# A fused attention, Fourier-mixing and feed-forward kernel: its planner gets a fitted transfer model, port rules and new durations

## Chip, core and metric

The kernel runs on 1 core of one Trainium2 chip. The metric is the device time of one execution in microseconds; the time of the kernel before is the median of three runs.

## What is computed

The reference, cut to what matters (batch 8, 8 heads, sequence 576, head size 64; x is [8, 576, 512]):

```python
rel = pos[:, None] - pos[None, :]
mask_plain = (rel >= 0) & (rel < 32)                       # heads 0 to 3
mask_dil = (rel >= 0) & (rel < 128) & (rel % 4 == 0)       # heads 4 to 7
scores = where(mask, q @ k.T / 8, -1e9)
x = softmax(scores) @ v                                    # heads side by side: [8, 576, 512]
u = x + real(fft(fft(x, axis=1), axis=2))
un = (u - mean(u)) / sqrt(var(u) + 1e-6)                   # over the last axis
out = u + maximum(un @ w_ch1, 0) @ w_ch2                   # 512 -> 2048 -> 512
```

## The kernel before

**Stages.** For each of 8 batches, attention runs in 12 small steps of two 96-row blocks for a pair of heads (`attend`, L513): TensorE multiplies queries and keys (L522), VectorE adds the mask and takes the row maximum in one operation (L530), ScalarE takes the exponential (L536), TensorE transposes it (L549) and multiplies it with the values (L556), VectorE divides by the sums (L564 to L568). `store` sends the result to folded scratch tensors in DRAM, `xsp` and `xsm` (L603). `mix` (L657) loads those folded tiles back (L675, L684, tiles `x0` to `x3`, `xt0`, `xt1`) and does the two Fourier transforms as products with constant cosine and sine tables `seq`, `chn`, `tail` and `alt`; float32 numbers are split into a high and a low part, and three products of parts make one. `normalise` (L614) makes the layer norm and stores u with its mean and scale.

The feed-forward layer has two parts. During attention, `fill` works through the first 5 of 16 slices of the hidden layer, two token tiles at a time, with `up` (L935) and `down` (L951), and `keep_part` stores the sums in `parts`. After that, 9 blocks of 512 tokens do the other 11 slices: `load_blocks` (L1065) turns the tokens (L1033, a VectorE transpose), makes four combinations (L1077) and splits seven operands into high and low parts in `xb` (L1087 on ScalarE, L1090 on VectorE or GpSimd); `two_tiles` (L1237) makes products by a seven-product scheme (L1209); `down` adds them up; `finish` (L972) adds the stored part, scales, adds u and writes the output rows. Weights come as 64-bit words that VectorE converts in five operations each (L866, L869, L872, L875, then L882 for the low part); those of the first slices are converted during attention, those of pair 3 and later during block 0.

**What sets the order.** Nothing in the code above runs in the order in which it is written. `Plan.add` records each step with an engine, a cost in us, a priority and its tiles; `Plan.run` (L235) then simulates the engines and the DMA queues with these costs and takes, whenever an engine is free, the ready step of the lowest priority. The instructions are emitted in that order, so each engine's queue is fixed by it, and at run time an engine goes through its queue in order and waits at each step. The priorities are the constants `P_...` and the step of the batch: 12 units for each batch. SyncE issues nearly all loads and stores, GpSimd those of the tables and the indirect ones. Before, a transfer is modelled like this:

```python
dma = max(dma, end + 0.65) + got.nbytes / 3.0e5
done = dma + 2.8
```

and GpSimd's table loads have no dependence but a time, `at=T_SEQ` or `T_CHN`, that exists in the plan alone; `start` (L450) writes them behind nothing on GpSimd's queue (L481, L483, L485, L486).

Of the kernel before, what the change touches and what calls it, by code (L numbers as in the profile page):

```python
# [173 lines left out]
class Op:  # L174
    __slots__ = ("eng", "cost", "fn", "prio", "bufs", "after", "waits", "ready", "start", "num", "nbytes")


class Plan:
# [1146 lines left out]
```

## Time and profile before

| | before |
|---|---|
| median of three runs (lowest, highest) | 1114.68 us (1114.53, 1117.69) |
| the profiled execution | 1114.71 us |
| its span | 1112.9 us |
| TensorE (PE) busy | 1064.3 us, 7066 matmuls |
| VectorE (DVE) busy | 726.0 us, 2318 instructions |
| ScalarE (ACT) busy | 522.2 us, 1331 instructions |
| GpSimd (POOL) busy | 288.7 us, 341 instructions |

The span is the time from the first to the last thing that the profiler saw; the execution's own time is 1.8 us longer. Busy times of the engines overlap. The granted clock (PEclk) is the share of full speed that TensorE was allowed: at 1.00 it runs at 2.4 GHz, and a mean between 0.5 and 1.00 says that it spent a part of the stretch at 1.2 GHz. DMA share is the mean busy share of the core's 16 DMA engines; overlapping transfers can bring it above 1.

### The profile page before, as it was taken

Reading aid. Unit: us, or ns where it says so; the run is one execution under the profiler, and the core shown is the slowest. Engines: PE = TensorE matmul, PEld = TensorE weight load, DVE = VectorE, ACT = ScalarE, POOL = GpSimd, SP = SyncE. Lnnn points to the kernel's source line nnn. Section 1 sums busy time; section 2 is a strip of 40 time slices with the busy share of each in tenths; the row PEclk is TensorE's granted clock in tenths of the full one; section 3 lists DMA queues with packets and bytes.
Section 4 is the critical chain, followed back from the end, with each engine's and each line's share of the span. In section 5 each row is a group of like instructions: output and inputs, shape, how many; then the busy total and the mean of one; then the engine's idle time right before and its main releaser. Section 6 shows DMA issues by size and latency. Waiting matters only on the chain.

```text
span 1112.9 us, 20217 instructions
## 1 busy us (share of the span) xinstructions
PE 1064.3 (96%) x7066; PEld 944.7 (85%) x7066; DVE 726.0 (65%) x2318; ACT 522.2 (47%) x1331; POOL 288.7 (26%) x341
## 2 busy tenths in 40 slices
PE   5799999999999999899989899999999999999997
PEld 3667888889898988899978798999998989899986
DVE  4789988777867878867769853536363545454523
ACT  3587756646554735334435443333333333333431
POOL 2015465443434344400040321121202120212200
PEclk9699999999999999999989999999999999999999
DMA  9667567756565344345523360505050504041211
GB/s 310 175 205 223 160 192 194 210 144 183 162 171 152 115 129 131 104 133 153 133 95 102 79 162 1 152 1 152 1 152 1 138 15 124 30 103 50 92 61 39
DMA packets 104310, 137.05 MB, mean 123 GB/s; under 512 B 9656, under 2 KB 62328, under 8 KB 104208
## 3 DMA queue, kind: packets, MB, share of 16 engines
q1 hardware_dynamic: 100624, 126.85, 40.6%
q0 software_dynamic: 3040, 8.09, 2.4%
q8 instruction: 56, 0.92, 0.4%
q10 hardware_dynamic: 544, 0.82, 0.2%
q14 instruction: 46, 0.38, 0.1%
HBM read 97.92 MB, written 37.80 MB: 122 GB/s over the span
## 4 chain that ended last, share of the span: by engine, by line
PE 80%; DVE 12%; DMA 3%; issue 2%; POOL 1%; ACT 1%; SPq 0%; DVEq 0%; ACTq 0%; POOLq 0%
PE sc L951 14%; PE ff L1209 13%; PE mix L1209 8%; PE ff L951 6%; PE ff L935 6%; PE pt L951 6%; PE av L951 6%; PE sc L522 6%; PE av L556 4%; PE mix L784 2%; PE mix L738 2%; PE pt L549 2%; PE pt L935 2%; DVE pm L530 1%; DMA ut<-in_w_dram 1%
## 5 line engine op out<-in xcount | busy, mean ns | idle before, releaser
L536 ACT ACTIVATE pm<-pm,mx 96x128 f32<-96x128 f32 x384 | 130.3, 394 | 54.2 <-DVE mx L530 50.6
L522 PE MATMUL sc<-kb,tq 128*96 128x256 f32 x384 | 110.1, 407 | 16.7 <-DMA kb<-in_k_dram 7.7
L1225 ACT COPY s<-ff 128x256 f32<-128x256 f32 x135 | 50.3, 374 | 159.2 <-PE ff L1209 158.9
L935 PE MATMUL ff<-ut,wa 128*128 128x256 f32 x780 | 109.0, 289 | 3.7 <-DVE h L943 3.6
L530 DVE CUSTOM_DVE_ANT_0 pm<-sc,mask_sb 96x128 f32<-96x128 f32 x384 | 92.8, 278 | 24.5 <-PE sc L522 23.9
L951 PE MATMUL sc<-wa,h 128*128 128x512 f32 x420 | 104.4, 391 | 0.0
L935 PEld LDWEIGHTS ff<-ut,wa 128*128 128x128 f32 x780 | 98.7, 192 | 5.7 <-DVE h L943 4.3
L951 PE MATMUL ff<-wa,h 128*128 128x512 f32 x390 | 93.8, 392 | 0.0
L556 PEld LDWEIGHTS av<-vt,ptsb 128*96 128x96 f32 x768 | 79.5, 170 | 16.2 <-issue 4.6
L1077 POOL TENSOR_TENSOR ut<-ut 128x512 f32<-128x512 f32 x36 | 50.6, 1426 | 160.3 <-DVE ut L1033 81.3
L556 PE MATMUL av<-vt,ptsb 128*96 128x65 f32 x768 | 84.4, 253 | 6.1 <-DVE xt L568 4.4
L951 PEld LDWEIGHTS sc<-wa,h 128*128 128x128 f32 x420 | 76.0, 188 | 13.8
L522 PEld LDWEIGHTS sc<-kb,tq 128*96 128x96 f32 x384 | 58.3, 174 | 30.6 <-DVE kb L465 7.7
L951 PE MATMUL sc<-wd,h 128*128 128x512 f32 x324 | 83.7, 393 | 0.0
L951 PEld LDWEIGHTS ff<-wa,h 128*128 128x128 f32 x390 | 71.6, 188 | 13.8
L1033 DVE STREAM_TRANSPOSE ut<-ut 128x512 f32<-128x512 f32 (+1 forms) x76 | 71.4, 980 | 13.6 <-DMA ut<-us 13.6
L1256 DVE TENSOR_TENSOR c<-s,s 128x256 f32<-128x256 f32 x45 | 22.2, 494 | 88.1 <-ACT s L1225 88.0
L1209 PEld LDWEIGHTS ff<-xb,pair 128*128 128x128 f32 x540 | 73.8, 188 | 6.4 <-ACT s L1225 0.7
L1209 PE MATMUL ff<-xb,pair 128*128 128x256 f32 x540 | 76.4, 280 | 0.5 <-ACT s L1225 0.5
L1090 POOL TENSOR_TENSOR xb<-ut,xb 128x512 fp32r<-128x512 f32 x27 | 36.9, 1367 | 132.1 <-ACT xb L1087 132.1
L1230 ACT ACTIVATE h<-row 128x256 fp32r<-128x256 f32 x90 | 37.5, 417 | 64.2 <-DVE row L1246 37.3
L989 POOL DMA_INDIRECT ut<-us,flip_sb x20 | 19.9, 996 | 183.8 <-DMA ut<-us 107.5
(158 smaller groups left out, 2312.2 us busy)
## 6 DMA issues: line engine op xcount, KB each, us to landing
vt<-in_v_dram SPq DMA_DIRECT2D x32, 390.0 KB
ut<-in_w_dram SPq DMA_DIRECT2D x20, 512.0 KB
us<-uc SPq DMA_DIRECT2D x36, 257.0 KB
tq<-in_q_dram SPq DMA_DIRECT2D x32, 288.0 KB
part<-row SPq DMA_DIRECT2D x36, 256.0 KB
ut<-us SPq DMA_DIRECT2D x36, 256.0 KB
ut<-part SPq DMA_DIRECT2D x36, 256.0 KB
kb<-in_k_dram SPq DMA_DIRECT2D x62, 144.0 KB
```

Of the source, the lines that this page charges most:

```text
L522: nc.tensor.matmul(sc()[:QB, 256 * n:256 * n + 256], lhsT=tq()[:, cols], rhs=kb()[:, :, keys], start=True, stop=True,)
L530: nc.vector.tensor_tensor_reduce(pm()[:, i], sc()[:QB, KB * i:KB * i + KB], mask_sb()[:, masks[blocks[i // 2]]], -0.125, 3.0e38, ALU.add, ...
L536: add("ACT", 0.295, lambda i=i: nc.scalar.activation(out=pm()[:, i], in_=pm()[:, i], func=AF.Exp, bias=mx()[:, i:i + 1], scale=-1.0), ((mx ...
L556: add("PE", 0.16, lambda i=i: nc.tensor.matmul(av()[:QB, 65 * i:65 * i + 65], lhsT=pt()[:, i], rhs=vt()[:, i % 2, blocks[i // 2]], start=T ...
L935: nc.tensor.matmul(z()[:, :n_tok], lhsT=wf()[:, a, kk], rhs=ut()[:, p, kk], start=(kk == 0 and n == 0), stop=(kk == KT - 1 and n == 2),)
L951: nc.tensor.matmul(acc(), lhsT=h()[:, a, P * s:P * s + P], rhs=wf()[:, p], start=(first and n == 0), stop=(last and n == 2),)
L1033: nc.vector.transpose(out=o[back], in_=x[:, g])
L1077: add("POOL", pool(C), lambda: nc.gpsimd.tensor_tensor(out=made(i)(), in0=x(), in1=y(), op=ALU.subtract), (*done, *((raw, ("s", j)) for j ...
L1090: add(eng, (pool if eng == "POOL" else dve)(C), lambda j=j, get=get, lo=lo: lo.tensor_tensor(out=xb()[:, j, 1], in0=get(), in1=xb()[:, j, ...
L1209: nc.tensor.matmul(z()[:, lo:lo + TOK1], lhsT=ap()[:, a, kk], rhs=xb()[:, j, p, kk], start=(start and k == 0), stop=(stop and k == 6 * len ...
L1225: add("ACT", act(TOK1), lambda: nc.scalar.copy(out=s(), in_=src()[:, :TOK1]), (src,), (s,), SOON - 1)
L1230: add("ACT", act(TOK1), lambda: nc.scalar.activation(out=h()[:, 0], in_=z(), func=AF.Relu), need, ((h, 0),), SOON)
```

## The change

The planner gets other numbers. A transfer now starts 0.83 us (SyncE, ScalarE) or 3.6 us (GpSimd) after its issue, moves 260 GB/s in place of 300, and lands 1.02 + 1.5 us later; rows of 2 KB count 0.52 of their bytes. Steps marked `port` (VectorE operations with two inputs in SBUF, and everything that GpSimd computes) exclude each other in the plan. Durations are changed (a VectorE transpose 1.0 in place of 0.6, matmuls and others by some per cent), and all priorities get new values.

Four things are changed beyond the order. Each table load of GpSimd gets a VectorE memset of one element of its tile ahead of it, on which it then depends. In the first block (XB = 1) `load_blocks` puts all combinations and splits on VectorE. In `finish` VectorE first makes u + part x scale, which doesn't need the accumulator, and then one scale-and-add from the accumulator, in place of an add of accumulator and part and a scale-and-add. SyncE's issue cost in the plan goes from 0.5 to 0.46.

```diff
-P_QK0, P_V0 = -8.0, -7.0
-P_ST, P_FD, P_WD, P_ST0, P_FD0, P_SPAN0, P_SPAN1 = -4.0, -12.0, -10.0, 0.0, 0.0, 8.0, 13.0
...
+P_ST, P_FD, P_WD, P_ST0, P_FD0, P_SPAN0, P_SPAN1 = -4.0, -21.87, -10.91, 0.0, 0.0, 23.02, 23.31
+P_QK, P_V, P_TR, P_MIX, P_SPAN, P_W, P_WF, P_FILL, P_FILLT = -8.0, -5.77, -5.0, 3.69, 13.04, 15.31, 8.7, 44.08, 3.7
+T_SEQ, T_CHN, T_STEP, P_SEQ, P_CHN = 7.07, 19.07, 0.08, -17.52, -2.0
+PAD_PE, PAD_DVE, PAD_ACT, PAD_POOL, LAND = 0.0, 0.0, 0.0, 0.0, 1.5
+XB = 1
...
+        op.port = port or (eng == "POOL" and not nbytes)
...
-                        if place(ops[e[1]], now):
+                        if (not ops[e[1]].port or port <= now) and place(ops[e[1]], now):
...
+                    if got.port:
+                        port = end
...
-                        dma = max(dma, end + 0.65) + got.nbytes / 3.0e5
-                        done = dma + 2.8
+                        dma = max(dma, now + LATE[eng]) + got.nbytes / 2.6e5
+                        done = dma + 1.02 + LAND
...
+LATE = {"SP": 0.83, "ACT": 0.83, "POOL": 3.6}
+ROW = 0.52
...
+        def table(t, m, dst, src, prio, nbytes, at):
+            def touch():
+                nc.vector.memset(dst().bitcast(F32)[0:1, 0:1] if m is None else dst().bitcast(F32)[0:1, 0, 0:1], 0.0)
+            key = t if m is None else (t, m)
+            add("DVE", 0.065, touch, (), (key,), prio, at=at)
+            add("POOL", 0.53, lambda: nc.gpsimd.dma_start(out=dst(), in_=src), (), (key,), prio, nbytes)
...
-        add("DVE", dve(C), lambda: nc.vector.tensor_tensor(
-            out=row(), in0=acc(), in1=row(), op=ALU.add), (acc,), (pk,), prio)
         add("DVE", 0.66, lambda: nc.vector.scalar_tensor_tensor(
-            row(), row(), u(C + 1, C + 2), u(0, C), op0=ALU.mult, op1=ALU.add), (uk,), (pk,), prio)
+            u(0, C), row(), u(C + 1, C + 2), u(0, C), op0=ALU.mult, op1=ALU.add), (pk,), (uk,), prio, port=True)
+        add("DVE", 0.66, lambda: nc.vector.scalar_tensor_tensor(
+            row(), acc(), u(C + 1, C + 2), u(0, C), op0=ALU.mult, op1=ALU.add), (uk, acc), (pk,), prio)
...
-                add("DVE", 0.6 / len(steps), lambda i=i, g=g, back=back: turn(i, g, back), raws, done[-1:], prio)
+                add("DVE", 1.0 / len(steps), lambda i=i, g=g, back=back: turn(i, g, back), raws, done[-1:], prio)
...
+        lone = c < XB
+        engine, name, cost = (nc.vector, "DVE", dve) if lone else (nc.gpsimd, "POOL", pool)
...
+            eng, lo, cost = ("POOL", nc.gpsimd, pool) if j in (3, 4, 6) and not lone else ("DVE", nc.vector, dve)
```

The order of VectorE around the first operation on a weight tile (`ut`, L866 before, L884 now; `pm` and `mx` are the masked scores and their maximum, `sums`, `rinv` and `xt` the finished output). Before:

```order
L564 TENSOR_SCALAR sums_317<-av_299 96x4
L567 RECIPROCAL rinv_322<-sums_317 96x4
L568 TENSOR_TENSOR xt_324<-av_299,rinv_322 96x4x64
L530 ISA pm_305,mx_306<-sc_293,mask_sb_160 96x128
L530 ISA mx_306 96x1
L530 ISA pm_305,mx_306<-sc_293,mask_sb_160 96x128
L530 ISA mx_306 96x1
L866 TENSOR_SCALAR ut_225<-ut_225 128x512
L530 ISA pm_340,mx_341<-sc_328,mask_sb_160 96x128
L530 ISA mx_341 96x1
L530 ISA pm_340,mx_341<-sc_328,mask_sb_160 96x128
```

Now:

```order
L586 TENSOR_TENSOR xt_340<-av_403,rinv_421 96x4x64
L582 TENSOR_SCALAR sums_434<-av_428 96x4
L585 RECIPROCAL rinv_437<-sums_434 96x4
L586 TENSOR_TENSOR xt_371<-av_428,rinv_437 96x4x64
L884 TENSOR_SCALAR ut_257<-ut_257 128x512
L887 SCALAR_TENSOR_TENSOR ut_257<-ut_257 128x512
L890 SCALAR_TENSOR_TENSOR ut_257<-ut_257 128x512
L893 SCALAR_TENSOR_TENSOR ut_257<-ut_257 128x512
L884 TENSOR_SCALAR ut_264<-ut_264 128x512
L887 SCALAR_TENSOR_TENSOR ut_264<-ut_264 128x512
L900 TENSOR_TENSOR wa1_0_150<-ut_257,wa1_0_150 128x512
L890 SCALAR_TENSOR_TENSOR ut_264<-ut_264 128x512
```

The first weight operation stood behind 16 masked maxima and alone among them. It now stands behind 24, and eight weight operations follow one another.

VectorE again, at the tokens of the first block (`xb` is written by the splits, L1090 before, L1111 now; L943 and L961 make the low half of h in the fills; L1098 are the combinations that GpSimd made before). Before:

```order
L1033 STREAM_TRANSPOSE ut_7818<-ut_7672 128x4x4x32 x3
L1090 TENSOR_TENSOR xb_7081<-ut_7818,xb_7081 128x512 x3
L866 TENSOR_SCALAR ut_7822<-ut_7822 128x512
L1090 TENSOR_TENSOR xb_7081<-ut_7672,xb_7081 128x512
L869 SCALAR_TENSOR_TENSOR ut_7822<-ut_7822 128x512
L872 SCALAR_TENSOR_TENSOR ut_7822<-ut_7822 128x512
L943 SCALAR_TENSOR_TENSOR h_7897<-pt_7867,h_7897 128x256
L875 SCALAR_TENSOR_TENSOR ut_7822<-ut_7822 128x512
L943 SCALAR_TENSOR_TENSOR h_7915<-av_7889,h_7915 128x256
```

Now:

```order
L1098 TENSOR_TENSOR ut_7653<-ut_7806 128x512
L961 SCALAR_TENSOR_TENSOR h_7922<-pt_7894,h_7922 128x256
L1098 TENSOR_TENSOR ut_7653<-ut_7806,ut_7653 128x512
L1111 TENSOR_TENSOR xb_7249<-ut_7653,xb_7249 128x512
L961 SCALAR_TENSOR_TENSOR h_7944<-av_7913,h_7944 128x256
L1111 TENSOR_TENSOR xb_7249<-ut_7653,xb_7249 128x512 x2
L961 SCALAR_TENSOR_TENSOR h_7969<-pt_7946,h_7969 128x256
L1111 TENSOR_TENSOR xb_7249<-ut_7806,xb_7249 128x512 x2
L1111 TENSOR_TENSOR xb_7249<-ut_7653,xb_7249 128x512
L884 TENSOR_SCALAR ut_7932<-ut_7932 128x512
L1111 TENSOR_TENSOR xb_7249<-ut_7806,xb_7249 128x512
L887 SCALAR_TENSOR_TENSOR ut_7932<-ut_7932 128x512
```

Four splits stood there, beside combinations and splits on GpSimd, with conversions of a weight tile between them and ahead of the next h. Now combinations and splits are all VectorE's, each h of the fills stands between them, and the weight tile comes behind.

SyncE where it first loads the folded tiles of batch 0 (L675 before, L693 now). Before:

```order
L505 DMA kb1_173<-in_k_dram 64x576 x2
L507 DMA tq_806<-in_q_dram 128x576
L508 DMA vt_813<-in_v_dram 128x780
L505 DMA kb2_174<-in_k_dram 64x576
L675 DMA x0_175<-xsp0_59 128x512
L675 DMA x2_177<-xsp0_59 128x512
L684 DMA xt0_179<-xsp0_59 32x512
L675 DMA x1_176<-xsm0_67 128x512
```

Now:

```order
L881 DMA ut_799<-in_w2_dram 128x512
L525 DMA tq_806<-in_q_dram 128x576
L693 DMA x0_175<-xsp0_59 128x512
L693 DMA x1_176<-xsm0_67 128x512
L523 DMA kb2_174<-in_k_dram 64x576 x2
L693 DMA x2_177<-xsp0_59 128x512
L621 DMA xsp1_60<-xt_758 96x2x256
L621 DMA xsp1_60<-xt_803 96x256
```

The loads of `x0` and `x1` stood behind the first half of the next keys, `kb2`, and behind the values `vt`. They now come ahead of `kb2`, and two weight tiles (L881) ahead of them.

## Rows read from the trace of the kernel before

**Rows 1.** The page's first section: busy us (share of the span) and instructions by engine.
```profile
PE 1064.3 (96%) x7066; PEld 944.7 (85%) x7066; DVE 726.0 (65%) x2318; ACT 522.2 (47%) x1331; POOL 288.7 (26%) x341
```

**Rows 2.** Table of stretches: length, busy PE, PEld, DVE, ACT, POOL (count), PEclk, DMA share, GB/s.
```profile
0.00:20.00 20.00, 10.17 (x56) 6.96 (x56) 10.13 (x61) 7.06 (x18) 5.75 (x14) 1.00 1.10 281
20.00:40.00 20.00, 14.07 (x56) 10.49 (x56) 14.26 (x60) 10.99 (x27) 0.00 (x0) 0.57 0.79 252
40.00:72.00 32.00, 27.20 (x163) 19.97 (x162) 22.43 (x127) 21.22 (x62) 0.12 (x1) 0.84 0.67 198
72.00:112.00 40.00, 36.44 (x284) 31.13 (x284) 35.78 (x188) 30.88 (x88) 21.43 (x29) 1.00 0.71 215
112.00:420.00 308.00, 304.03 (x2266) 269.87 (x2265) 243.57 (x1114) 178.27 (x494) 132.72 (x190) 1.00 0.59 166
420.00:476.00 56.00, 51.49 (x329) 45.99 (x328) 47.55 (x101) 22.26 (x52) 20.95 (x26) 0.97 0.39 111
560.00:588.00 28.00, 22.30 (x145) 20.71 (x144) 18.50 (x31) 12.48 (x32) 8.49 (x6) 0.88 0.25 85
616.00:644.00 28.00, 24.95 (x143) 22.13 (x142) 21.22 (x35) 12.35 (x29) 12.90 (x9) 0.94 0.35 81
644.00:1092.00 448.00, 448.00 (x2841) 404.13 (x2841) 215.83 (x414) 173.12 (x413) 82.73 (x67) 1.00 0.28 75
1092.00:1112.90 20.90, 13.72 (x78) 11.68 (x76) 7.63 (x14) 1.57 (x4) 0.00 (x0) 0.88 0.18 51
```

**Rows 3.** TensorE's waits: line waited for, us in total, times, longest us.
```profile
PE sc L522 <- DMA kb<-in_k_dram: 7.7, 1, 7.7
PE sc L522 <- DVE mx L530: 7.6, 5, 4.5
PE pt L935 <- DVE h L943: 5.2, 1, 5.2
...
PE ff L935 <- DVE h L943: 3.6, 2, 2.8
...
PE ff L1209 <- ACT h L1230: 3.1, 1, 3.1
```

**Rows 4.** Timeline 0 to 24 us: start, us, engine, line, op [idle <-releaser].
```profile
1.25 1.29 POOL L481 DMA_DIRECT2D seq<-in_seq_dram  x2 [0.82 <-POOLq L1313]
...
22.70 0.43 DVE L866 TENSOR_SCALAR ut<-ut 128x512 uint32<-128x512 uint32 x1 [4.36 <-DMA ut<-in_w_dram]
...
23.60 1.17 PE L522 MATMUL sc<-kb,tq 128*96 128x256 f32 x2 [4.53 <-DVE mx L530]
```

**Rows 5.** Transfers issued from 0 to 60 us: KB each, median us to landing.
```profile
seq<-in_seq_dram POOLq DMA_DIRECT2D x4, 290.0 KB, 7.2
```

**Rows 6.** Table of stretches, columns as in rows 2, the first 8 us.
```profile
0.00:4.00 4.00, 0.00 (x0) 0.00 (x0) 2.58 (x15) 1.28 (x1) 2.94 (x9) 1.00 0.56 148
4.00:8.00 4.00, 0.30 (x1) 0.33 (x2) 2.34 (x9) 0.00 (x0) 2.13 (x5) 1.00 1.21 289
```

**Rows 7.** VectorE by line, 20 to 64 us: count | busy us, mean ns | idle.
```profile
L869 DVE SCALAR_TENSOR_TENSOR ut<-ut 128x512 uint32<-128x512 uint32 x5 | 3.4, 681 | 0.0
```

**Rows 8.** VectorE by line, 100 to 560 us, columns as in rows 7.
```profile
L1033 DVE STREAM_TRANSPOSE ut<-ut 128x512 f32<-128x512 f32 (+1 forms) x40 | 37.7, 984 | 13.6 <-DMA ut<-us 13.6
```

**Rows 9.** VectorE by line and shape, 555 to 572 us, columns as in rows 7.
```profile
L1090 DVE TENSOR_TENSOR xb<-ut,xb 128x512 fp32r<-128x512 f32 x4 | 5.8, 1500 | 0.1
...
L869 DVE SCALAR_TENSOR_TENSOR ut<-ut 128x512 uint32<-128x512 uint32 x1 | 1.7, 1746 | 0.0
...
L875 DVE SCALAR_TENSOR_TENSOR ut<-ut 128x512 f32<-128x512 f32 x1 | 1.4, 1420 | 0.0
```

**Rows 10.** Timeline of the end, columns as in rows 4.
```profile
1105.78 4.23 SPq L1008 DMA_DIRECT2D out_dram<-ut  x8
...
1107.53 1.41 DVE L997 SCALAR_TENSOR_TENSOR ut<-ut 128x512 f32<-128x512 f32 x2
```

**Rows 11.** Waits of SyncE's queue, columns as in rows 3.
```profile
SPq L675 <- DVE uc L619: 13.8, 13, 3.1
```

More of the change, by code (lines that the diff above doesn't have):

```diff
@@ L174 @@
 class Op:
-    __slots__ = ("eng", "cost", "fn", "prio", "bufs", "after", "waits", "ready", "start", "num", "nbytes")
+    __slots__ = ("eng", "cost", "fn", "prio", "bufs", "after", "waits", "ready", "start", "num", "nbytes", "port")
 class Plan:
     LAG = {"PE": 0.2, "DVE": 0.13, "ACT": 0.155, "POOL": 0.08, "SP": 0.05, "NONE": 0.0}
+    PAD = {"PE": PAD_PE, "DVE": PAD_DVE, "ACT": PAD_ACT, "POOL": PAD_POOL, "SP": 0.0, "NONE": 0.0}
     OWN = {"PE": 0.0, "DVE": 0.13, "ACT": 0.155, "POOL": 0.08, "SP": 0.05, "NONE": 0.0}
@@ L251, in run @@
         lanes = {e: [] for e in busy}
+        port = 0.0
         def place(o, now):
@@ L636, in turned @@
         for kk in range(KT):
-            add("PE", 0.109, lambda kk=kk: nc.tensor.transpose(
+            add("PE", 0.12, lambda kk=kk: nc.tensor.transpose(
                 tp()[:, P * kk:P * kk + P], uc()[:, kk:C:KT],
@@ L684, in fold @@
                     dma(lambda x=x, src=src, lo=lo, p0=p0, k=k: nc.sync.dma_start(
-                        out=x()[p0:p0 + k, 0:C], in_=src()[lo:lo + k]), (src,), ((x, key),), early, k * 2048)
+                        out=x()[p0:p0 + k, 0:C], in_=src()[lo:lo + k]), (src,), ((x, key),), early, k * 2048 * ROW)
             t1, t2 = work("t1", [P, NEH], F32, 1), work("t2", [P, NEH], F32, 1)
@@ L911, in combine @@
             add("DVE", dve(256), lambda: nc.vector.tensor_tensor(out=made(i)(), in0=x(), in1=y(), op=op),
-                need + tuple((t0, ("s", j)) for j in after), ((t0, ("s", i)),), prio)
+                need + tuple((t0, ("s", j)) for j in after), ((t0, ("s", i)),), prio, port=True)
         if n == 1:
@@ L1008, in put @@
                     queues[e][0].dma_start(out=out[2 * pair + e, lo:lo + 32], in_=row()[p0:p0 + 32])
-                add(queues[e][1], 0.5, put, (pk,), (), prio, 32 * 2048)
+                add(queues[e][1], 0.5, put, (pk,), (), prio, 32 * 2048 * ROW)
             return
@@ L1074, in made @@
             return lambda: words(raw)[:, C * i:C * i + C].rearrange("p (k t) -> p k t", k=2)
+        lone = c < XB
+        engine, name, cost = (nc.vector, "DVE", dve) if lone else (nc.gpsimd, "POOL", pool)
         def combine(i, x, y, after=()):
-            add("POOL", pool(C), lambda: nc.gpsimd.tensor_tensor(out=made(i)(), in0=x(), in1=y(), op=ALU.subtract),
-                (*done, *((raw, ("s", j)) for j in after)), ((raw, ("s", i)),), prio)
+            add(name, cost(C), lambda: engine.tensor_tensor(out=made(i)(), in0=x(), in1=y(), op=ALU.subtract),
+                (*done, *((raw, ("s", j)) for j in after)), ((raw, ("s", i)),), prio, port=True)
         combine(0, plain(0, 1), plain(0, 0))
@@ L1226, in snap, with put_h @@
         return s
-    def put_h(z, need):
+    def put_h(z, need, port=True):
         h = hidden()
@@ L1256, in two_tiles @@
         add("DVE", dve(TOK1), lambda: nc.vector.tensor_tensor(
-            out=c22(), in0=s3(), in1=s5(), op=ALU.add), (s3, s5), (c22,), SOON)
+            out=c22(), in0=s3(), in1=s5(), op=ALU.add), (s3, s5), (c22,), SOON, port=True)
         h22 = put_h(lambda: c22(), (c22,))
```

93 lines of the change are left out of this document (46 added, 47 removed).

## The prediction

> **What bounds the kernel now.** I read the page's busy shares first: TensorE is busy for 96% of the span [rows 1]. So time can only come out of what TensorE doesn't do: standing still, and running at the lower of its two clock levels (1.2 against 2.4 GHz). The second view, the table of stretches, says where that is [rows 2]. I count for each stretch the idle time and, beside it, busy time x (1 - granted clock). 0 to 20 us: 9.8 idle. 20 to 40: 5.9 idle and 14.07 x 0.43 = 6.1 by the clock. 40 to 72: 4.8 and 4.4. 72 to 112: 3.6 idle. 112 to 420: only 4.0 in 308 us. 420 to 476: 4.5 and 1.5. 560 to 588: 5.7 and 2.7. 616 to 644: 3.1 and 1.5. 644 to 1092: nothing. 1092 to the end: 7.2 and 1.6. Together 66 us. The 448 us of whole blocks near the back have nothing to give, so a new order matters in the first 112 us, at two places between 420 and 644 us, and at the very end.
>
> The third view, TensorE's waits, names who is late there [rows 3]: the first keys (7.7 us), VectorE's masked maximum (4.5 us at once), and VectorE's second half of h (5.2 and 2.8) or ScalarE's h behind it (3.1). TensorE is the bound, and most of its holes are a late VectorE queue.
>
> **The change part by part.** Work on TensorE is the same, instruction for instruction; only the order moves. The sum is made against the profiled execution, 1114.71 us with a span of 1112.9; the median of the three runs, 1114.68, is the same number.
>
> *A, first keys.* Before, GpSimd's queue issues the constant tables from 1.25 us on, two issues in 1.29 us [rows 4]: 4 x 290 KB [rows 5] and, by their shapes, 4 x 258, 435 and 129, together 2.76 MB. They run beside the first keys and queries (2 x 144 + 288 = 576 KB by their shapes), which let TensorE start only at 7.7 us [rows 3]. Now a one-element VectorE memset stands before each table's issue, behind the memsets of the key buffers, so that the tables start near 7 us. In the first 4 us the queues moved 148 GB/s, 0.59 MB, and from 4 to 8 us 289 GB/s, 1.16 MB [rows 6]: the 576 KB alone would be through at 4.0. They still share with mask, permutation and values of their own queue, 0.7 us more at the second rate for some 0.2 MB of these. I take 4.7, a gain of 3.0. Bounds: 0 and 3.7.
>
> *B, the first weights.* VectorE reaches its first weight operation after 16 mask operations and stands 4.36 us for the landing; TensorE waits 4.53 behind it [rows 4]. Now 24 mask operations and more finished outputs come first (see the order of VectorE), so the landing should be over. But eight weight operations then stand in one piece, two of 0.43 [rows 4] and six of 0.68 [rows 7], 4.9 us, while TensorE can only fill the free score banks. I take a gain of 2. Bounds: 0 and 4.4.
>
> *C, the lower clock at 20 to 72 us.* 6.1 + 4.4 = 10.5 us are lost by busy time at the lower level [rows 2]. It follows stalls that the change shortens but does not remove. I take half, 5. Bounds: 0 and 10.5.
>
> *D, the other early holes.* Idle of 20 to 112 us, without the 3.6 us of B's wait that lie in it: 5.9 + 4.8 + 3.6 - 3.6 = 10.7 [rows 2]. Fewer weight operations stand between the masks up to the 40th (10 against 20 by the order). A quarter: 2.7. Bounds: -3 (new holes as large as those of 72 to 112) and 7.
>
> *E, 420 to 476 us.* The planner priced a VectorE transpose at 0.6 us; the rows show 0.98 for 40 of them [rows 8]. So it filled VectorE's queue beyond what fits, and h came late (2.8 us) [rows 3]. Now it is priced at 1.0, and two-input VectorE operations and GpSimd's exclude each other in the plan. Half of the 6.0 lost there: 3. Bounds: -3 and 6.
>
> *F, block 0's tokens, 560 to 644 us.* Between 555 and 572 us VectorE's operations beside GpSimd's took 1.50 us (four of them), 1.75 and 1.42 [rows 9], where 0.68 is what the size takes alone [rows 7]: 4 x 0.82 + 1.07 + 0.74 = 5.1 us too long, as much as the h behind them made TensorE wait, 5.2 [rows 3]. Block 0's four combinations and three splits now leave GpSimd. VectorE gets 7 x 0.68 = 4.8 us of work, no more than it no longer loses, and it stood for 28.0 - 18.5 = 9.5 us in 560 to 588 [rows 2]. Block 0's products also move behind all of the fills. Of 8.4 us lost in the first stretch I take 7.5, and 2.5 of the 4.6 in 616 to 644, where block 1 still uses GpSimd: 10. Bounds: 2 and 13.
>
> *G, the block's end.* After the last accumulators VectorE has eight operations for four tiles, an add and a scale-and-add each, until 1107.53 + 1.41 = 1108.94; the output issues begin at 1105.78 and need 4.23 us for eight [rows 10]. Now the scale-and-add of the stored part runs earlier, and four operations remain. The first comes out one add sooner, so the issues begin at about 1104.5 and are the limit: 1.3 us less. Bounds: 0 and 2.2 (all of VectorE's tail).
>
> The other edits cost nothing that I can place. Ten memsets of one element lie in VectorE's 9.9 idle us of the first 20 [rows 2]; without that cover they cost at most ten times the 0.43 of a 512-element operation, 4.3. A margin on landings moves an instruction back in its queue; it does not itself wait.
>
> Sum: 3.0 + 2.0 + 5.0 + 2.7 + 3.0 + 10.0 + 1.3 = 27.0, and 1114.7 - 27.0 = 1087.7, so **1088 us**.
>
> **Rivals.** *R1, the start is paid back.* The DMA engines are loaded through the first 20 us (share 1.10 [rows 2]); the tables are not fewer, only later, and meet the weights and the second pair's loads. What is won at 7.7 us is lost at the next landing, and the lower clock of 20 to 40 us stays. A to D (12.7) fall away: 1087.7 + 12.7 = 1100. For it: the share. Against it: VectorE no longer stands in front of the late landing. The Trainium skill, "DMA: Bandwidth & Descriptors", section "SWDGE vs HWDGE vs iDMA", says that queues fed by software (GpSimd's) and by hardware (SyncE's) are different ones and that each DMA engine takes turns between them; by that rule the tables at 7 us again take their turns against the weights, which would be R1's result, 1100, and the load share agrees that no room is free. I give R1 0.22.
>
> *R2, the middle doesn't move.* A faster start only brings VectorE's backlog of weights, transposes and normalisation forward; it is busy for 47.55 of 56 us in 420 to 476 [rows 2], and E and F go to zero: 1087.7 + 13 = 1101. Against it: F's loss has a named cause that is taken out. 0.15.
>
> *R3, slower: SyncE's queue.* The loads of the folded tiles get their due time 21.87 instead of 12 units ahead, and so stand before loads of keys and queries (see SyncE's order). They wait until a tile is free: 13 waits, 13.8 us, the longest 3.1 [rows 11]. If in each of the seven later batches the two pairs of loads stand for that longest wait, SyncE loses 7 x 2 x 3.1 = 43 us and attention starves with it: 1087.7 + 43 = 1131. It decides once a batch costs TensorE 27 / 7 = 3.9 us more. Against it: two query buffers lie between. 0.10.
>
> *R4, nothing arrives*: the new order differs, but the holes only change places, 1114. 0.06.
>
> **How the numbers follow.** The forecast has 0.47. About 0.3% (3.3 us) is what a measurement of this kernel can tell from no change. Forecast, R1 and R2 are faster: 0.84. R4 is the same: 0.06. R3 is slower: 0.10. The range: all upper bounds together give 3.7 + 4.4 + 10.5 + 7 + 6 + 13 + 2.2 = 46.8, which is 1068; all of them at once is unlikely, and I begin at 1073. At the other end it takes in R1 and R2, with the negative ends of D and E: 1108. R3, R4 and a small rest lie outside, 0.2.
>
> **What would show it.** The first score product near 4.7 us; no wait of VectorE for weights at 20 us; a granted clock over 0.8 in 20 to 40 us; no wait for h of 2 us or more between 420 and 644; VectorE's xb operations of the first block near 0.68 us; VectorE's last operation some 2 us sooner after the last product. The forecast is wrong if TensorE's waits list keys, queries or values in attention (R3), or if the first 112 us hold as much idle time as now (R1).

## The result, and the profile after

| | before | changed |
|---|---|---|
| median | 1114.64 us | 1099.14 us |
| lowest, highest of four | 1114.53, 1117.69 | 1096.97, 1101.75 |
| the profiled execution, its span | 1114.71, 1112.9 | 1098.52, 1096.7 |

The ratio is 0.9855 with a 95% interval of 0.9828 to 0.9883: 15.5 us faster, where 27 were forecast; 1099.1 lies inside the stated range.

The products of the blocks are the same in both kernels, so their starts in the timeline cut the two spans into equal pieces of work. In each of the two views below, one line is the first product of block 0, the next the first product of block 1, and the last line holds the last matmuls of all. Before:

```profile
561.66 0.87 PE L1209 MATMUL ff<-xb,pair 128*128 128x256 f32 x6
...
640.54 0.88 PE L1209 MATMUL ff<-xb,pair 128*128 128x256 f32 x6
...
1104.88 0.84 PE L951 MATMUL av<-wa,h 128*128 128x512 f32 x3
```

After, with two more lines ahead that give the price of work which stood behind block 0's first product before and stands ahead of it now:

```profile
546.83 6.98 PE L969 MATMUL sc<-wa,h 128*128 128x512 f32 x30
553.64 1.58 PE L953 MATMUL pt<-ut,wa 128*128 128x256 f32 x12
...
567.51 0.88 PE L1230 MATMUL ff<-xb,pair 128*128 128x256 f32 x6
...
622.73 0.88 PE L1230 MATMUL ff<-xb,pair 128*128 128x256 f32 x6
...
1090.60 0.84 PE L969 MATMUL av<-wa,h 128*128 128x512 f32 x3
```

That work is 30 matmuls of `down` (6.8 us from the first start to the next line's) and 36 of `up` (three groups of 1.42 us, start to start): 11.1 us. With it moved to the same side:

| piece | before | after | difference |
|---|---|---|---|
| up to block 0's first product | 561.66 + 11.1 = 572.8 | 567.5 | -5.3 |
| block 0 | 78.88 - 11.1 = 67.8 | 55.2 | -12.6 |
| blocks 1 to 8, to TensorE's last matmul (1105.72, 1091.44) | 465.2 | 468.7 | +3.5 |
| after it | 7.2 | 5.3 | -1.9 |
| span | 1112.9 | 1096.7 | -16.2 |

The table of stretches after (columns as in rows 2) answers to [rows 2]:

```profile
0.00:20.00 20.00, 11.93 (x76) 8.93 (x76) 12.92 (x87) 9.86 (x28) 3.07 (x9) 1.00 1.01 273
20.00:40.00 20.00, 14.22 (x67) 9.89 (x68) 12.86 (x64) 9.89 (x27) 2.65 (x5) 0.66 0.83 261
40.00:72.00 32.00, 26.47 (x184) 19.77 (x185) 26.55 (x142) 24.59 (x68) 2.01 (x2) 0.94 0.72 222
72.00:112.00 40.00, 39.31 (x302) 33.90 (x302) 35.96 (x194) 32.41 (x89) 16.69 (x24) 0.96 0.74 223
112.00:420.00 308.00, 301.59 (x2226) 266.97 (x2225) 237.30 (x1065) 174.23 (x478) 128.57 (x181) 1.00 0.56 161
420.00:476.00 56.00, 52.12 (x343) 46.64 (x342) 48.36 (x100) 22.34 (x53) 25.99 (x33) 1.00 0.39 110
560.00:588.00 28.00, 27.99 (x182) 25.19 (x181) 27.66 (x62) 16.49 (x41) 0.00 (x0) 1.00 0.46 151
616.00:644.00 28.00, 28.00 (x179) 25.11 (x179) 20.68 (x35) 13.12 (x31) 10.66 (x9) 1.00 0.64 169
644.00:1092.00 448.00, 445.75 (x2799) 400.19 (x2797) 227.60 (x402) 165.37 (x399) 85.89 (x66) 1.00 0.25 67
```

560 to 644 us lost 13.0 us before and loses nothing now. The first 112 us lost 34.6 (9.8 + 12.0 + 9.2 + 3.6) and still lose 28.1 (8.1 + 10.6 + 7.1 + 2.3). 112 to 420 us lose 6.4 where they lost 4.0, 420 to 476 lose 3.9 where they lost 6.0. The last row loses 2.3 us, 0.6 of them behind TensorE's last matmul and the rest in blocks that stood full before. Of the 3.5 us that blocks 1 to 8 lose by their starts, 2.2 lie in block 7, which took 60.0 us in place of 57.8.

TensorE's waits after (columns as in rows 3):

```profile
PE sc L540 <- DMA kb<-in_k_dram: 6.9, 1, 6.9
...
PE ff L953 <- DVE h L961: 3.9, 4, 1.4
```

The waits of 4.5, 5.2, 2.8 and 3.1 us [rows 3] are gone. The first keys are still 6.9 us late. The end (timeline; VectorE's last operation and SyncE's issues answer to [rows 10]):

```profile
1089.44 1.43 DVE L1015 SCALAR_TENSOR_TENSOR ut<-sc,ut 128x512 f32<-128x512 f32 x2 [3.93 <-PE sc L969]
...
1090.22 3.60 SPq L1026 DMA_DIRECT2D out_dram<-ut  x8
...
1091.48 0.75 DVE L1015 SCALAR_TENSOR_TENSOR ut<-av,ut 128x512 f32<-128x512 f32 x1
```

The first operation on an accumulator already gives an output row, and VectorE ends 0.8 us after TensorE's last matmul, where it ended 3.2 us after it.

### The profile page after: what moved, and what is told of

Read it like the earlier page. It is cut to its first block, busy times and chain, and to the rows that moved or that the text cites. A ratio compares the mean times of both kernels' runs of the same rounds, so it can differ in the third digit from the quotient of the medians.

```text
span 1096.7 us, 20233 instructions
## 1 busy us (share of the span) xinstructions
PE 1059.4 (97%) x7066; PEld 938.5 (86%) x7066; DVE 742.9 (68%) x2335; ACT 520.9 (47%) x1331; POOL 283.1 (26%) x334
## 4 chain that ended last, share of the span: by engine, by line
PE 80%; DVE 11%; DMA 3%; ACT 2%; issue 2%; SPq 1%; POOL 0%; ACTq 0%; DVEq 0%; POOLq 0%
PE sc L969 14%; PE ff L1230 12%; PE mix L1230 7%; PE sc L540 7%; PE ff L953 7%; PE ff L969 6%; PE av L969 5%; PE pt L969 5%; PE av L574 5%; PE mix L756 3%; PE mix L802 3%; PE pt L567 3%; PE pt L953 2%; DMA ut<-us 2%; DVE pm L548 2%
## 5 line engine op out<-in xcount | busy, mean ns | idle before, releaser
L953 PE MATMUL ff<-ut,wa 128*128 128x256 f32 x780 | 106.8, 287 | 4.2 <-DVE h L961 3.9
L1098 POOL TENSOR_TENSOR ut<-ut 128x512 f32<-128x512 f32 x32 | 49.5, 1566 | 186.1 <-DVE ut L1051 185.5
L574 PEld LDWEIGHTS av<-vt,ptsb 128*96 128x96 f32 x768 | 77.1, 167 | 21.3 <-ACT ptsb L570 8.9
L574 PE MATMUL av<-vt,ptsb 128*96 128x65 f32 x768 | 82.1, 249 | 8.8 <-ACT ptsb L570 4.4
L969 PEld LDWEIGHTS sc<-wa,h 128*128 128x128 f32 x420 | 76.0, 188 | 13.8
L1277 DVE TENSOR_TENSOR c<-s,s 128x256 f32<-128x256 f32 x45 | 26.7, 594 | 77.5 <-ACT s L1246 77.5
L540 PEld LDWEIGHTS sc<-kb,tq 128*96 128x96 f32 x384 | 57.9, 173 | 24.0 <-issue 6.8
L1230 PE MATMUL mix<-xb,pair 128*128 128x256 f32 x486 | 65.1, 278 | 0.8 <-DVE row L1284 0.8
L969 PEld LDWEIGHTS sc<-wd,h 128*128 128x128 f32 x324 | 56.9, 188 | 9.6 <-DVE h L1253 0.3
```

The source lines that it names most:

```text
L540: nc.tensor.matmul(sc()[:QB, 256 * n:256 * n + 256], lhsT=tq()[:, cols], rhs=kb()[:, :, keys], start=True, stop=True,)
L574: add("PE", 0.17, lambda i=i: nc.tensor.matmul(av()[:QB, 65 * i:65 * i + 65], lhsT=pt()[:, i], rhs=vt()[:, i % 2, blocks[i // 2]], start=T ...
L953: nc.tensor.matmul(z()[:, :n_tok], lhsT=wf()[:, a, kk], rhs=ut()[:, p, kk], start=(kk == 0 and n == 0), stop=(kk == KT - 1 and n == 2),)
L969: nc.tensor.matmul(acc(), lhsT=h()[:, a, P * s:P * s + P], rhs=wf()[:, p], start=(first and n == 0), stop=(last and n == 2),)
L1098: add(name, cost(C), lambda: engine.tensor_tensor(out=made(i)(), in0=x(), in1=y(), op=ALU.subtract), (*done, *((raw, ("s", j)) for j in af ...
L1230: nc.tensor.matmul(z()[:, lo:lo + TOK1], lhsT=ap()[:, a, kk], rhs=xb()[:, j, p, kk], start=(start and k == 0), stop=(stop and k == 6 * len ...
```

## The experiments

Where the text says "same plan", only what a step issues is changed and every engine's order stays; "planned anew" means that the order can move anywhere. The changed kernel and three kernels with its order unchanged up to block 0 (the old block end, all blocks on VectorE, and block 0 on GpSimd, all below) started their last score product at 393.7, 394.8, 395.3 and 397.1 us, so single profiles differ by some us that are nobody's edit; medians and pieces are compared. The kernel before, run again beside each of the three groups of experiments, had medians of 1114.4, 1113.2 and 1113.6 us; the changed kernel was not run again, so about 1 us of a difference to its 1099.1 can be drift.

### Block 0's combinations and splits

```diff
-        engine, name, cost = (nc.vector, "DVE", dve) if lone else (nc.gpsimd, "POOL", pool)
+        engine, name, cost = (nc.gpsimd, "DVE", dve) if lone else (nc.gpsimd, "POOL", pool)
...
+            lo = nc.gpsimd if j in (3, 4, 6) else lo
```

> The changed kernel, every step in the same place of the plan, but block 0's four combinations and three splits are carried out by GpSimd again. Theory 1 (the gain before block 1, some 12.6 us by the starts of the blocks, comes from GpSimd's neighbourhood being gone): VectorE's splits and weight steps near 560 us take 1.3 us and more again, TensorE waits 8 to 12 us there, time about 1107 to 1111 us. Rival 2 (the gain comes from the fills being placed ahead of all products of block 0): TensorE loses at most 3 us there, time 1099 to 1102 us.

Median 1106.34 us, 7.2 more than the changed kernel. The four splits that stayed on VectorE took 0.68 us, but five weight steps between 554 and 564 us took 1.52 to 1.78 us beside GpSimd, where their sizes take 0.42 to 0.69 alone; the last two of them are the line below. TensorE waited once for h (VectorE by line and shape, 560 to 590 us, then TensorE's waits, 540 to 640 us):

```profile
L893 DVE SCALAR_TENSOR_TENSOR wst<-wst 128x512 f32<-128x512 f32 x2 | 3.5, 1726 | 0.0
```

```profile
PE pt L953 <- DVE h L961: 3.4, 1, 3.4
```

From the last score product to block 0's first product this kernel took 576.32 - 397.07 = 179.3 us, the changed one 567.51 - 393.72 = 173.8, and the other two of the same plan 172.9 and 173.0: 5.5 us are shown at the place. So theory 1 is right in kind, and the effect is smaller than it said. The other way round, in the kernel before:

```diff
+            lo = nc.vector if c == 0 else nc.gpsimd
-            add("POOL", pool(C), lambda: nc.gpsimd.tensor_tensor(out=made(i)(), in0=x(), in1=y(), op=ALU.subtract),
+            add("POOL", pool(C), lambda: lo.tensor_tensor(out=made(i)(), in0=x(), in1=y(), op=ALU.subtract),
...
-            lo = nc.gpsimd if eng == "POOL" else nc.vector
+            lo = nc.gpsimd if eng == "POOL" and c else nc.vector
```

> The kernel before, every step in the same place of its plan, but block 0's combinations and splits are carried out by VectorE. Theory 1: the h behind them is no longer late, 8 to 12 us are won between 555 and 640 us, time about 1103 to 1107 us. Rival 2: the seven operations stand in VectorE's queue in front of the same h, TensorE waits about as long as before, time 1111 to 1115 us.

Median 1110.04 us, 4.3 less than before on the same chip, ratio 0.9962 (0.9948 to 0.9975); between the two theories. Every split took its size's time (VectorE, 552 to 572 us), and the wait of 5.2 us became 1.8, while the 3.1 behind it stayed (TensorE's waits, 540 to 660 us):

```profile
L1091 DVE TENSOR_TENSOR xb<-ut,xb 128x512 fp32r<-128x512 f32 x7 | 4.5, 684 | 0.0
```

```profile
PE ff L1210 <- ACT h L1231: 3.1, 1, 3.1
PE pt L935 <- DVE h L943: 1.8, 1, 1.8
```

So freeing VectorE of GpSimd is a third of the 12.6 us in the old order, and nearly half in the new one; the rest came with the new order, which has the fills' products and h's ahead of the weights and of block 0's products. No run takes that order apart.

### The port rule in the plan

```diff
-        op.port = port or (eng == "POOL" and not nbytes)
+        op.port = False
```

> The changed kernel planned without the rule that two-input VectorE operations and GpSimd exclude each other; durations and priorities stay. Theory 17 (the rule keeps h on time): TensorE's waits for h between 112 and 480 us grow from 3.9 to 7 us or more, and the blocks lose more than their 3.5 us, time 1102 to 1106 us. Rival 18 (the true durations alone do it): time 1097 to 1101 us.

Median 1108.36 us, 9.2 more than the changed kernel, more than theory 17 gave the rule. But the place was another one. Waits for h in the fills grew only from 3.9 to 4.2 us; block 0 took 62.1 us in place of 55.2, with a wait for h of its own products and the lower clock behind it (TensorE's waits and the stretch, 600 to 660 us):

```profile
PE ff L1230 <- DVE h L1253: 3.4, 1, 3.4
```

```profile
600.00:660.00 60.00, 56.12 (x332) 49.69 (x332) 47.55 (x73) 25.04 (x58) 18.14 (x13) 0.94 0.47 120
```

3.9 us idle and 56.12 x 0.06 = 3.4 by the clock. In front of that h, between 615 and 625 us, six VectorE operations beside GpSimd's took 5.8 us more than their sizes take alone (an h 1.52 and 1.49 us in place of 0.42, a weight step 1.77 in place of 0.69); in front of the same h of the changed kernel two did, by 1.5 us. Blocks 1 to 8 took 469.2 us, hardly more than with the rule (468.7). The rest was lost before block 0: 112 to 420 us lose 11.5 us in place of 6.4, though no wait of TensorE there is over 1.6 us. Since everything is planned anew, how much of the 9.2 us is the rule itself and how much another order stays open.

### Blocks 1 to 8 and the block's end

The early scale-and-add (L1013) has both inputs in SBUF, as the late one of before had (L997). VectorE by line, 690 to 1050 us, before and after:

```profile
L997 DVE SCALAR_TENSOR_TENSOR ut<-ut 128x512 f32<-128x512 f32 x25 | 18.1, 745 | 0.0
```

```profile
L1013 DVE SCALAR_TENSOR_TENSOR ut<-ut 128x512 f32<-128x512 f32 x26 | 31.4, 1223 | 0.3 <-ACT ut L1010 0.2
```

The mean of 1.22 us mixes two kinds. 12 of the 26 run while GpSimd makes combinations, and took 1.78 us each; the other 14 run without GpSimd and took 0.75, as in the old place. One pair of the first kind, with GpSimd beside it, and one operation of the second (timelines of the changed kernel, GpSimd and VectorE by themselves):

```profile
702.65 6.13 POOL L1098 TENSOR_TENSOR ut<-ut 128x512 f32<-128x512 f32 x4 [9.82 <-DVE ut L1051]
```

```profile
704.14 3.48 DVE L1013 SCALAR_TENSOR_TENSOR ut<-ut 128x512 f32<-128x512 f32 x2
```

```profile
741.29 0.75 DVE L1013 SCALAR_TENSOR_TENSOR ut<-ut 128x512 f32<-128x512 f32 x1
```

The Trainium skill, "SBUF — State Buffer", section "Who interferes with whom", says that a VectorE instruction with two SBUF inputs contends with a GpSimd instruction that reads SBUF, and one with at most one SBUF input doesn't, unless it runs in a mode that uses both ports. L1013 agrees with the first half. The late operation (L1015, one input from the accumulator) can't bear on the second, because 23 of its 24 executions in these 360 us run without GpSimd. The h of the blocks can: both of these run beside GpSimd's combinations (612.06 to 619.42 us), the first with its input `row` in SBUF, the second with `ff`, the accumulator.

```profile
615.05 1.51 DVE L1253 SCALAR_TENSOR_TENSOR h<-row,h 128x256 fp32r<-128x256 f32 x1
616.49 0.41 DVE L1253 SCALAR_TENSOR_TENSOR h<-ff,h 128x256 fp32r<-128x256 f32 x1
```

Two experiments on L1013, both of the same plan. First the old block end in the late place:

```diff
-            u(0, C), row(), u(C + 1, C + 2), u(0, C), op0=ALU.mult, op1=ALU.add), (pk,), (uk,), prio, port=True)
+        add("DVE", 0.66, lambda: None, (pk,), (uk,), prio, port=True)
...
+            nc.vector.tensor_tensor(out=row(), in0=acc(), in1=row(), op=ALU.add)
+            nc.vector.scalar_tensor_tensor(row(), row(), u(C + 1, C + 2), u(0, C), op0=ALU.mult, op1=ALU.add)
```

> The changed kernel with the old block end: VectorE does the add from the accumulator and the scale-and-add one after the other, both in the late place; the early place is empty. Theory 3 (blocks 1 to 8 became 3.5 us longer because the early scale-and-add runs beside GpSimd's combinations, 1.22 us in place of 0.75): every block is 57.8 us again, the end is 1.9 us longer, time 1.6 us shorter, about 1097.5. Rival 4 (the blocks lose by another part of the new order): blocks keep their 57.8 to 60.0 us, and with the longer end the time is about 1101 us.

Median 1106.89 us, 7.8 slower: theory 3 falls as it was put. Blocks 2 to 6 took 58.9 to 59.1 us, although L1017 was back at 0.75. The late place now holds eight operations, six of them in a row for 4.2 us, where the plan counted one for each tile. TensorE waits for h behind them (640 to 1040 us), and the tail after TensorE's end is 7.2 us, as before:

```profile
PE sc L969 <- DVE h L1255: 2.9, 6, 0.5
```

So in this order an early operation that is sometimes slowed is cheaper than a second late one. That holds for this order only: in the kernel before, whose own plan had both operations late, the blocks took 57.8 us, and the old block end with a plan made for it under the new rules was not run. Then the neighbour taken away, in all nine blocks:

```diff
-        engine, name, cost = (nc.vector, "DVE", dve) if lone else (nc.gpsimd, "POOL", pool)
+        engine, name, cost = (nc.vector, "DVE", dve) if lone else (nc.vector, "POOL", pool)
...
+            lo = nc.vector
```

> The changed kernel, every step in the same place of the plan, but the combinations and splits of all nine blocks are carried out by VectorE, so that GpSimd computes nothing beside it there. Theory 3: the early scale-and-add takes 0.75 us, blocks 1 to 8 are 57.8 us each, time 3.5 us shorter, about 1095.6. Rival 5 (VectorE becomes late where seven more operations, 4.8 us in each block, stand in its queue ahead of an h): blocks longer than 58.5 us, time 1103 us or more.

Median 1096.88 us, 2.3 less than the changed kernel; the two ratios to before (0.9823 to 0.9860, against 0.9828 to 0.9883) overlap, so the time alone doesn't show it. The place does: no L1013 takes more than 0.77 us, and blocks 1 to 6 took 57.8 to 57.9 us (block 7, with 58.9, still loses one):

```profile
L1013 DVE SCALAR_TENSOR_TENSOR ut<-ut 128x512 f32<-128x512 f32 x27 | 19.7, 746 | 1.8 <-ACT ut L1010 1.8
```

Blocks 1 to 8 took 466.6 us: 2.1 of the 3.5 us are GpSimd's neighbourhood. No run explains the other 1.4, most of which lie in block 7.

### The tables and the first keys

Without the ten memsets, same plan:

```diff
             def touch():
-                nc.vector.memset(dst().bitcast(F32)[0:1, 0:1] if m is None else dst().bitcast(F32)[0:1, 0, 0:1], 0.0)
+                pass
```

> The changed kernel, same plan, without the ten memsets ahead of the table loads, so that GpSimd issues all tables from about 1.3 us on, as before. Theory 6: first score product at 6.2 to 7.7 us as in the runs so far of either kind; the time is 1097 to 1101 us. Rival 8 (holding the tables back is worth its part of the start): first product at 7.5 us or later, more idle time in the first 40 us, time 1102 us or more.

Median 1104.01 us, 4.9 more: rival 8. Holding the tables back is worth its part, though only little of it at the keys, which landed at 7.5 us. The next queries were late too: TensorE waits 1.0 us for them at 15.5 us, as the kernel before does for 1.2 us, and it does so in none of the profiles with the memsets.

```profile
0.00:20.00 20.00, 10.06 (x61) 7.51 (x62) 11.15 (x71) 8.67 (x24) 5.75 (x14) 1.00 1.08 289
20.00:40.00 20.00, 14.25 (x70) 10.20 (x69) 12.48 (x55) 9.74 (x26) 0.00 (x0) 0.61 0.65 211
40.00:72.00 32.00, 28.16 (x178) 21.12 (x176) 22.85 (x137) 22.89 (x66) 1.80 (x2) 0.87 0.70 214
72.00:112.00 40.00, 38.27 (x276) 32.16 (x277) 36.31 (x185) 32.12 (x89) 15.24 (x22) 0.91 0.74 217
```

By idle time and clock: 9.9, 11.3, 7.5 and 5.2, together 33.9 in place of 28.1. What the keys have for company instead:

```diff
+            for _ in range(4):
+                nc.gpsimd.memset(mask_sb(), 0.0)
```

> The changed kernel with the mask's load, and all that stands behind it on SyncE's queue, held back by four GpSimd memsets of the mask tile, some 2 to 4 us, so that only the first keys and queries (576 KB) are under way at first. Theory 6 (the tables were never what made the first keys late; SyncE's own next loads, mask, permutation, values, identity, share the engines with them): first score product at 5.0 us or earlier, in place of 6.87. Rival 7 (the first keys need that long by themselves): first product at 6.2 us or later.

The first product came at 5.55 us, between the two (timeline): the loads that share the queue are a part, 0.6 to 1.3 us against the 6.2 to 6.9 of the kernels of the same plan. It was executed once only, in 1096.55 us.

```profile
5.55 1.99 PE L544 MATMUL sc<-kb,tq 128*96 128x256 f32 x4 [5.55 <-DMA kb<-in_k_dram]
```

And the tables later still:

```diff
-T_SEQ, T_CHN, T_STEP, P_SEQ, P_CHN = 7.07, 19.07, 0.08, -17.52, -2.0
+T_SEQ, T_CHN, T_STEP, P_SEQ, P_CHN = 30.0, 45.0, 0.08, -17.52, -17.52
```

> The changed kernel with the tables planned later: seq and tail at 30 us, chn and alt at 45 us of the plan (planned anew). Theory 9 (the chn tables issued at 20.9 us meet queries and weights at full load, queries land only at 25.2 us, and TensorE drops to the lower clock): idle time and time lost by the clock in 20 to 40 us fall from 10.6 to under 6, time 3 to 5 us shorter, 1094 to 1096. Rival 10 (the eight weight operations that stand in one piece make the stall and the clock): 20 to 40 us lose 9 us or more still, time 1098 to 1101.

Median 1097.88 us, 1.3 less, inside the spread. 20 to 40 us lose 2.8 + 17.21 x 0.17 = 5.7 us, as theory 9 said, but the run doesn't decide between it and rival 10: the new plan moved the weights too, and six of the eight operations now run from 19.95 to 24.2 us, ahead of the next scores. And 40 to 72 gave it back, 8.8 + 23.18 x 0.21 = 13.7 where 7.1 were lost. TensorE waits there for finished outputs of VectorE (`xt`), whose queue holds other weight operations between 42.82 and 49.0 us; no transfer is named (stretches, then TensorE's waits, 40 to 72 us):

```profile
20.00:40.00 20.00, 17.21 (x106) 13.04 (x106) 17.16 (x96) 14.75 (x41) 2.89 (x5) 0.83 0.63 198
40.00:72.00 32.00, 23.18 (x133) 16.94 (x132) 24.25 (x115) 18.34 (x49) 4.07 (x7) 0.79 0.88 256
```

```profile
PE av L574 <- DVE xt L586: 6.9, 4, 2.6
```

### The priorities

All that the kernel before has by name are back, the rest is as changed; the new ones of the table loads, P_SEQ and P_CHN, stay:

```diff
-P_QK0, P_V0 = -7.8, -7.0
+P_QK0, P_V0 = -8.0, -7.0
...
-P_QK, P_V, P_TR, P_MIX, P_SPAN, P_W, P_WF, P_FILL, P_FILLT = -8.0, -5.77, -5.0, 3.69, 13.04, 15.31, 8.7, 44.08, 3.7
+P_QK, P_V, P_TR, P_MIX, P_SPAN, P_W, P_WF, P_FILL, P_FILLT = -8.0, -7.0, -5.0, 2.0, 13.0, 8.0, 8.0, 45.0, 4.0
```

> The changed kernel's planner, durations, port rule, touches, block end and block 0 on VectorE, but with the old values of all priorities (planned anew; the times for the tables stay). Theory 11 (rules, durations and the four changes beyond the order bring the gain): time at most 1103 us. Rival 12 (the new priorities bring it): time 1108 us or more, the difference before block 0's first product.

Median 1091.91 us (1089.61 to 1095.46), ratio to before 0.9801 (0.9778 to 0.9824): 7.2 us better than with the new values. Theory 11 holds, and more: the new priorities cost time. Which of them? The folded loads first.

```diff
-P_ST, P_FD, P_WD, P_ST0, P_FD0, P_SPAN0, P_SPAN1 = -4.0, -21.87, -10.91, 0.0, 0.0, 23.02, 23.31
+P_ST, P_FD, P_WD, P_ST0, P_FD0, P_SPAN0, P_SPAN1 = -4.0, -12.0, -10.91, 0.0, 0.0, 23.02, 23.31
```

> The changed kernel with the one priority of the folded tiles' loads back at -12 (planned anew). Theory 13 (SyncE stands for a free tile at these loads, 25.1 us in all in the changed kernel against 13.8 before, and this makes attention's loads late): these waits fall to about 14 us and the time is 3 to 6 us shorter, 1093 to 1096. Rival 14 (SyncE's queue has the room): time 1097 to 1101 us.

Median 1096.76 us, 2.4 less; the intervals (0.9828 to 0.9876, against 0.9828 to 0.9883) don't part the two. SyncE's wait hardly moved (changed, then this one), so theory 13 isn't borne out:

```profile
SPq L693 <- DVE uc L637: 25.1, 12, 8.7
```

```profile
SPq L693 <- DVE uc L637: 23.2, 13, 7.7
```

Then the priorities of the first weights (P_WD goes to -10 as well):

```diff
-P_QK, P_V, P_TR, P_MIX, P_SPAN, P_W, P_WF, P_FILL, P_FILLT = -8.0, -5.77, -5.0, 3.69, 13.04, 15.31, 8.7, 44.08, 3.7
+P_QK, P_V, P_TR, P_MIX, P_SPAN, P_W, P_WF, P_FILL, P_FILLT = -8.0, -5.77, -5.0, 3.69, 13.04, 8.0, 8.0, 44.08, 3.7
```

> The changed kernel with the three priorities of the first weights back at 8, 8 and -10 (planned anew): the first weight operations stand behind 18 and 24 masked maxima in place of both behind 24. Theory 15 (the later weights, in one piece, are what the new priorities cost): 20 to 72 us lose 5 us less than the 17.7 of the changed kernel, time 1091 to 1095 us. Rival 16 (another priority costs it): time 1097 to 1101 us.

Median 1091.13 us (1089.58 to 1095.17, all below the changed kernel's lowest, 1096.97), 8.0 less than the changed kernel: theory 15. The ratios to before, 0.9780 to 0.9836 against 0.9828 to 0.9883, just touch. The timeline of the changed kernel shows the price, VectorE's weight operations from 24.48 us on and the masked maximum behind them:

```profile
24.48 0.41 DVE L884 TENSOR_SCALAR ut<-ut 128x512 uint32<-128x512 uint32 x1
...
25.24 2.88 PE L540 MATMUL sc<-kb,tq 128*96 128x256 f32 x6 [1.54 <-DMA tq<-in_q_dram]
...
29.33 0.28 DVE L548 CUSTOM_DVE_ANT_0 pm<-sc,mask_sb 96x128 f32<-96x128 f32 x1
...
30.11 0.71 PE L567 MATMUL pt<-perm_sb,pm 96*128 96x96 f32 x2 [2.00 <-ACT pm L554]
```

The scores of 25.24 us on wait while VectorE is 4.85 us in weights. With the old values these operations stand among the masks from 18 maxima on and are over at 25.7 us, before the next scores begin at 26.35; 20 to 112 us lose 7.3 + 4.3 + 0.4 = 12.0 in place of 20.0 (table of stretches):

```profile
20.00:40.00 20.00, 15.27 (x96) 11.28 (x95) 14.89 (x82) 11.92 (x34) 2.65 (x5) 0.83 1.02 312
40.00:72.00 32.00, 27.66 (x202) 20.99 (x200) 29.37 (x161) 26.40 (x74) 5.14 (x8) 1.00 0.76 226
72.00:112.00 40.00, 39.65 (x321) 34.11 (x322) 36.79 (x198) 32.09 (x91) 18.08 (x26) 1.00 0.78 241
```

Of these 8.0 us, 2.6 are idle time and 5.4 the clock. The clock had fallen by 26 us in both kernels, so the piece of weights is not what made it fall. But here TensorE then worked without a hole, and the higher level was back in 30 to 32 us; in the changed kernel TensorE stood 2.00 us behind the masks, as the line at 30.11 shows, and the level came back only in 36 to 38 us:

```profile
30.00:32.00 2.00, 2.00 (x17) 1.75 (x17) 0.96 (x9) 1.71 (x6) 0.00 (x0) 0.93 1.10 375
```

```profile
36.00:38.00 2.00, 2.00 (x9) 1.38 (x8) 0.51 (x4) 0.69 (x2) 0.00 (x0) 0.57 0.35 83
```

The old priorities as a whole don't show the same in their one profile, which is the slowest of their four executions (1095.46 us). There the second tile's weights stand in one piece again, from 24.90 to 28.9 us, TensorE waits 2.25 us behind them, and 20 to 112 us lose 18.8 us; in the profile of the next section, with the same priorities, they lose 20.7. So the weights are what this one edit wins, and what else the old priorities win is open.

```profile
29.70 1.30 PE L567 MATMUL pt<-perm_sb,pm 96*128 96x96 f32 x4 [2.25 <-ACT pm L554]
```

### Three findings together

The old priorities and the held first loads, as above, and all blocks on VectorE, planned anew:

```diff
-XB = 1
+XB = 9
```

> Three findings together: the changed kernel with the old priorities, all nine blocks' combinations and splits on VectorE (both planned anew), and four GpSimd memsets that hold the mask's load and those behind it until the first keys are under way. If the three add up: 1091.9 less some 2 for the blocks and less 0 to 1 for the keys, 1088 to 1091 us. If VectorE becomes late in the fills or blocks with GpSimd's work: 1093 us or more.

Median 1090.35 us (1087.30 to 1091.65), ratio to before 0.9780 (0.9754 to 0.9806), the fastest median of all and 8.8 us under the changed kernel. Blocks 1 to 6 took 57.8 to 57.9 us. That it beats the old priorities alone (1091.9) or the old weights alone (1091.1) is not shown: the ranges overlap.

## Why the prediction was right or wrong

The sign and the range were right, the size was not: 27.0 forecast, 15.5 measured. By the pieces of the two profiles, A to E were to give 15.7 us before block 0's first product, and 5.3 came; F was to give 10, and 12.6 came; G 1.3, and 1.9 came; blocks 1 to 8 were to stay as they were, and lost 3.5. That the sum came no further off is in part luck, since F and G gave 3.2 us more than was put. Of its signs, the first product at 4.7 us (it came at 6.87) and the clock over 0.8 in 20 to 40 us (0.66) failed. By its steps:

- **F** (10 taken, bounds 2 to 13): 12.6. Right, splits at 0.68 us and no wait for h there, as it said. Its cause was put too simply: VectorE freed of GpSimd gives 4.3 us alone in the old order, and the rest came with the new one.
- **G** (1.3): 1.9 at the tail, where four scale-and-adds follow the last products in place of eight operations. Against the last product the issues begin 1.3 us sooner, as it said, and they took 3.60 us for eight, not 4.23.
- **Blocks 1 to 8** were costed at nothing ("nothing to give"): +3.5. This is the step that failed on the minus side. G moved a two-input VectorE operation beside GpSimd's combinations, the very neighbourhood that F prices at 0.8 us an operation, and the sum didn't apply it there; it cost 1.0 us (1.78 - 0.75) where the two met, and 2.1 of the 3.5 us came back with GpSimd out of the blocks.
- **B to D** (2 + 5 + 2.7): 20 to 112 us lost 24.8 us and lose 20.0, so 4.8 of the 9.7. Idle time fell from 14.3 to 12.0 us, where B and D put 4.7, and the loss by the clock from 10.5 to 8.0, where C put 5. The step that failed on the plus side is B, and C with it. B's own 4.9 us of weight operations in one piece was right to 0.1, and so was the row in the order; it was weighed against the wait of 4.53 that went, and still booked as a gain of 2, and C halved the loss by the clock as if this piece made no new stall. With the weights among the masks again, planned anew, the same stretch gives another 8.0.
- **A** (3.0): the keys landed 0.8 us sooner in the profile. Even that is not shown to be the change's, since the kernel before with block 0 on VectorE, whose start is the old one, had its first product at 6.74 us. The memsets are worth 4.9 us in the whole, but through the first 112 us together (the next queries 1.0 us sooner are one part), not through the keys; the rest of the mechanism stays open.
- **E** (3): 420 to 476 us gave 2.1, and 112 to 420 took 2.4 back. Nothing in sum. The port rule counted to E is worth 9.2 us with all that its plan moves, in block 0 and from 112 to 420 us.

Of the rivals, R1's 1100 is near the time, yet its ground is not what happened: holding the tables back gained 4.9 us, and the loss came by VectorE's queue. The rule that the Trainium skill states ("DMA: Bandwidth & Descriptors", section "SWDGE vs HWDGE vs iDMA") would have had that gain at nothing; the run decides. Where tables were moved again, 4.9 us were won in 20 to 40 us and 6.6 lost in 40 to 72, but that loss stands behind VectorE's weights, 6.9 us of waits for `xt`, and not at a landing. R2 is out, since F came in full. R3's waits did grow, 13.8 to 25.1 us with a longest of 8.7 [rows 11], but TensorE's waits name queries once, 1.5 us, and no cost of it could be shown. R4 is out.

## What to carry to other kernels

Price an operation where it will stand: an edit that takes a two-input VectorE operation off the end and puts it beside GpSimd's work can pay there what the end saves (here 2.1 us in the blocks against 1.9 at the end). When a table of priorities and several real changes come together, run the real changes with the old table too: here that came to 1091.9 us, and the new table gave 7 us of it back. Work in one piece on a queue costs the engine that waits behind it at the moment when its data is ready, not the idle time that the queue has on average.
